# A planned attention and feed-forward kernel: small VectorE operations go to GpSimd and ScalarE, and the planner counts VectorE's waits for GpSimd

## The chip, the core and the metric

The kernel runs on one core of a Trainium2 chip. A core has a matrix engine (TensorE, PE in the profile), VectorE (DVE), ScalarE (ACT), GpSimd (POOL) and SyncE (SP), which issues the transfers. Each engine takes its instructions in the order in which they were written, and waits on semaphores for what other engines make. The metric is device time of one execution, in microseconds (us); lower is better.

## The reference

Three stages, 4608 tokens of 512 numbers:

```
k_p, v_p = means of k, v over 8 neighbours          # 576 -> 72 places, 8 batches, 8 heads of 64
attn = softmax(q @ k_p.T / 8) @ v_p                 # the row sum gets + 1e-9
x = attn as 4608 x 512
h = x @ w_in                                        # 512 -> 1024
solu = h * softmax(h)
ln = (solu - mean) / sqrt(var + 1e-6) * g_ln
y = ln @ w_out                                      # 1024 -> 512
h2 = y @ w2_in                                      # 512 -> 2048
out = (h2 * sigmoid(1.702 * h2)) @ w2_out           # 2048 -> 512
```

## The kernel before

The program has two parts that follow each other on PE. The **first part** does attention, the first feed-forward stage with its norm, and the splitting of all weights. The **second part** does the last feed-forward stage over 12 blocks of 384 tokens; nothing of it is touched here, and its products go to `bank_a`, `bank_b` and `bank_d`.

Products are made in float16 from a high and a low half, so each float32 operand is scaled by a power of two, cast (`hi`), and subtracted (`lo`). The powers of two come from a small chain: largest magnitude of a tile per partition (`am`), spread over partitions by putting it on a diagonal (`diag = eye * am`) and multiplying by ones on PE, a maximum over the row (`alln`), the exponent bits (`pw`), and a few one-column operations (`rc`, `up`, `dn`). Function `largest` holds the diagonal, `whole_scale` and `wide_scale` the one-column operations.

The first part works on 36 tiles of 128 tokens. For each tile `attention` loads `qt`, multiplies it with the pooled keys (`kbd`) into the bank `psx`, takes the row maxima (`mx`), subtracts and exponentiates (`e`), sums the rows (`rs`: a reduction, a scaling `(rs + 1e-9) / A_TOP`, a reciprocal), normalises `e`, splits it into `st`, turns it by a transposing transfer (`aT`), multiplies with the values (`vst`) into the one bank `psv`, and reads that bank twice, on ACT and on DVE, into `xT`. `Pair.hidden` multiplies `xT` with `w1i` into `psh` (two buffers), and makes `hmx`, `nm`, `he`, `tt`, the sum `sm`, the `mean` and the sum of squares `vs`. `Pair.norm` makes, for two tiles together, on 128x2 values, the factor `a` and the shift `mean` of the norm: `q`, `v`, then a power -0.5 on GpSimd (`r`), one correcting step (`q`, `q`, `a`), `mean`. ACT then applies `a` and `mean` to `tt`, casts it (`zs`), GpSimd subtracts the low half, and a transposing transfer makes `zT`, which `project` multiplies with `w1o` into `psy`. Between these, the weights of the last stage are loaded (`raw`), joined from 64-bit input, combined (`w_f`), split and stored.

The order of the first part's instructions isn't written out. Each piece of work is a strand of operations with a due time, and `Plan.run` builds the order: at each step it estimates when the next operation of each strand could start, from its own model of engine costs (`cost`) and of latencies between engines, and writes out the one with the lowest start, shifted a little by its due time. `V`, `G`, `A` put an operation on DVE, POOL, ACT; `VG` lets the plan choose between POOL and DVE. So a cost in the model changes the order on every engine. Due times and their constants (`STEP`, `LAG_PROJECT` and others) stay as they are. Almost all first-part vector work is recorded under one helper line, L472, and its products under L501; the names of the tiles tell the operations apart.

Of the kernel before, what the change touches and what calls it, by code (L numbers as in the profile page):

```python
# [13 lines left out]
ALU = mybir.AluOpType  # L14
# [62 lines left out]
TOP3 = 2.0 ** -29 * (1 - 2.0 ** -23)  # L77
A_TOP = 2.0 ** 14
LN_UP = 2.0 ** 10
SQ_DOWN = 1.0 / (LN_UP * math.sqrt(DF1))  # L80
V_MOST = 2.0 ** 100
Y_TOP = 2.0 ** 13
G_DOWN = 2.0 ** -22
TINY = 2.0 ** -100
# [15 lines left out]
class Op:  # L100


    def __init__(self, engines, emit, outs, ins, cost, turn=False):
        self.engines, self.emit, self.cost, self.turn = engines, emit, cost, turn
        self.outs, self.ins = ([Region(x) for x in xs] for xs in (outs, ins))


# [65 lines left out]
class Plan:  # L173
# [7 lines left out]
    def __init__(self):  # L181
        self.free = dict.fromkeys(("pe", "dve", "act", "pool", "sp", "dma", "none"), 0.0)
        self.uses, self.floor, self.rings, self.ring_of = {}, {}, {}, {}
        self.strands, self.now, self.warm = [], None, 0.0

    def start(self, steps, due):
        s = Strand(self, steps, due)
# [16 lines left out]
    def drop(self, *tiles):  # L204
        for t in tiles:
            del self.ring_of[t.name]
# [12 lines left out]
    def estimate(self, op):  # L219
        best = None  # L220
        for engine in op.engines:
            t = max(self.free[engine], self.ready(op, engine))
            if engine == "sp":
                t = max(t, self.free["dma"] - 2000)
            key = t + op.cost[engine] + self.spare[engine] if len(op.engines) > 1 else t
            if best is None or key < best[0]:
                best = (key, t, engine)
        return best[1:]

    def take(self, op, t, engine):  # L230
        if engine == "sp":
            begin = max(self.free["dma"], t + (1275 if op.turn else 1100))
            self.free["dma"] = end = begin + op.cost["sp"]
            self.free["sp"] = max(t + 625, end - 920) if op.turn else t + 520
            engine = "dma"
        elif engine == "none":
            return
        else:
            cost = op.cost[engine]
            if engine == "pe":  # L240

                gap = t - self.free["pe"]
                self.warm = 0.0 if gap > 3400 else self.warm if gap < 300 or self.warm > 3400 else 0.0
                if self.warm < 3400:
                    cost = min(2 * cost, 3400 - self.warm + max(0.0, cost - (3400 - self.warm) / 2))
                self.warm += cost
            self.free[engine] = end = t + cost
        for regions, writes in ((op.ins, False), (op.outs, True)):
            for r in regions:
                u = self.uses.setdefault(r.name, [])  # L250
                u[:] = [x for x in u if not (x[1] == writes and x[0].box == r.box and x[3] == engine)]
                u.append((r, writes, end, engine))
# [25 lines left out]
def moe_kernel(ctx: ExitStack, tc: tile.TileContext, qT, kT, vT, w_in, w_out, g_ln, w2_in, w2_out, eye, outT):  # L278
# [135 lines left out]
    with ExitStack() as ph:  # L414
# [54 lines left out]
        def op(engines, name, args, kw):  # L469
            def emit(engine):  # L470
                eng = {"dve": nc.vector, "pool": nc.gpsimd, "act": nc.scalar}[engine]
                getattr(eng, name)(*args, **kw)  # L472

            kw_out = [kw[k] for k in ("out", "accum_out") if k in kw]
            outs = aps(kw_out or args[:1])
            ins = aps([v for k, v in kw.items() if k not in ("out", "accum_out")] + list(args[0 if kw_out else 1 :]))
            return Op(engines, emit, outs, ins, {e: cost(e, name, outs, ins) for e in engines})

        def V(name, *args, **kw):
            return op(("dve",), name, args, kw)  # L480
# [49 lines left out]
        def largest(am, alln, least, early=True):  # L530


            if early:
                diag = yield New(sb, [P, P], F32, "diag0", "y", 2)
            else:
                diag = yield New(kv, [P, P], F32, "diag", bufs=1)
            yield V("tensor_scalar", out=diag, in0=eye_t, scalar1=am, scalar2=least, op0=ALU.mult, op1=ALU.max)
            yield there(diag)
            if early:
                ps = yield New(psy, [P, 2, YB], F32, "psy", "psy")  # L540
            else:
                ps = yield New(psv, [P, DM], F32, "psv", "psv")
            spread = ps[:, 0, :P] if early else ps[:, :P]
            yield T([(spread, ones, diag, True, True)])
            drop(diag)
            yield V("tensor_reduce", out=alln, in_=spread, axis=AX.X, op=ALU.max)
            drop(ps)

        def exponent(pw, alln):
            yield V(  # L550
# [17 lines left out]
        def wide_scale(alln, up, dn, there_now):  # L568
            pw, rc = s1("pw", 1, KM), s1("rc", 1, KM)
            yield from exponent(pw, alln)  # L570
            yield V("reciprocal", rc, pw)
            yield V("tensor_scalar_mul", up, rc, 2.0 ** -111)
            there_now.add((up.name, up.offset))
            yield V("tensor_mul", rc, pw, pw)
            yield V("tensor_mul", rc, rc, rc)
            yield V("scalar_tensor_tensor", out=dn, in0=rc, scalar=2.0 ** -8, in1=rc, op0=ALU.mult, op1=ALU.mult)

        def values_of(raw, up, dst, begun=None):

# [28 lines left out]
        def whole_scale(alln, up, dn):  # L608

            pw, rc = s1("pw", 1, KM), s1("rc", 1, KM)  # L610
            yield from exponent(pw, alln)
            yield V("reciprocal", rc, pw)
            yield V("tensor_mul", rc, rc, rc)
            yield V("tensor_mul", rc, rc, rc)
            yield V("scalar_tensor_tensor", out=up, in0=rc, scalar=2.0 ** 8, in1=rc, op0=ALU.mult, op1=ALU.mult)
            yield V("reciprocal", dn, up)

        def joined(raw, measured):
# [141 lines left out]
        def keys(b, due):  # L760
            kp = yield from pooled("k", b, kT, due)
            yield lambda: b < 2 or scored[last_tile(b - 2)]
            for j in range(2):
                r = slice(j * D64, (j + 1) * D64)
                yield V(
                    "tensor_scalar_mul", kbd[b % 2][r, :, j * SP : (j + 1) * SP], kp[r],
                    1.0 / (NPOOL * math.sqrt(D64)),
                )
            drop(kp)
            k_ready[b] = True  # L770

        def values(b, due):
# [17 lines left out]
            v_ready[b] = True  # L790
            yield w_in_done.over
            both = s1("v_sc", 2)
            yield V(
                "scalar_tensor_tensor", out=both[:, 0:1], in0=dn, scalar=1.0 / NPOOL, in1=w1i_dn, op0=ALU.mult,
                op1=ALU.mult,
            )
            yield V(
                "scalar_tensor_tensor", out=both[:, 1:2], in0=up, scalar=float(NPOOL), in1=w1i_up, op0=ALU.mult,
                op1=ALU.mult,
            )  # L800
            for t in range(NTILE):
                for o, n, tb in spans(t):
                    if tb == b:
# [3 lines left out]
        def attention(t):  # L807
# [40 lines left out]
                yield A(out=e, in_=e, func=AF.Exp)  # L848
            rs = s1("rs", H)
            yield V("tensor_reduce", out=rs, in_=e, axis=AX.X, op=ALU.add)  # L850
            yield V("tensor_scalar", out=rs, in0=rs, scalar1=1e-9, scalar2=1.0 / A_TOP, op0=ALU.add, op1=ALU.mult)
            yield V("reciprocal", rs, rs)
            yield VG("tensor_tensor", out=e, in0=e, in1=rs.unsqueeze(2).to_broadcast([P, H, SP]), op=ALU.mult)
            yield lambda: t < 2 or turned[t - 2]
# [40 lines left out]
        class Pair:  # L895
# [7 lines left out]
            def hidden(self, j):  # L903
# [10 lines left out]
                for k in range(KM):  # L914
# [26 lines left out]
                    accum_out=self.mean[:, s],  # L941
                )
                drop(ps)
                yield V("tensor_scalar_mul", self.mean[:, s], self.mean[:, s], -SQ_DOWN / DF1)
                yield A(
                    out=e, in_=tt, func=AF.Square, scale=SQ_DOWN, bias=self.mean[:, s], accum_out=self.vs[:, s]
                )
                drop(e)
                self.tt[j] = tt

            def norm(self):
# [3 lines left out]
                self.a = a  # L955


                tiny = 1e-6 * DF1 * SQ_DOWN ** 2
                yield V("scalar_tensor_tensor", out=q, in0=self.sm, scalar=1e-9, in1=self.ci, op0=ALU.add, op1=ALU.mult)
                yield V("scalar_tensor_tensor", out=q, in0=q, scalar=tiny, in1=q, op0=ALU.mult, op1=ALU.mult)  # L960
                yield V("scalar_tensor_tensor", out=v, in0=q, scalar=V_MOST, in1=self.vs, op0=ALU.min, op1=ALU.add)
                yield G("tensor_tensor", out=r, in0=v, in1=minus_half, op=ALU.pow)
                yield V("tensor_mul", q, r, r)
                yield V("scalar_tensor_tensor", out=q, in0=q, scalar=-0.5, in1=v, op0=ALU.mult, op1=ALU.mult)
                yield V("scalar_tensor_tensor", out=a, in0=q, scalar=1.5, in1=r, op0=ALU.add, op1=ALU.mult)
                yield V(
                    "scalar_tensor_tensor", out=self.mean, in0=self.mean, scalar=1.0 / SQ_DOWN, in1=a, op0=ALU.mult,
                    op1=ALU.mult,
                )
                yield lambda: self.i == 0 or pairs[self.i - 1].zT is not None  # L970
                self.zT = yield New(sb, [P, 2 * K1, YB], F16, "zT", "zT", 2)
                for j in range(2):
# [501 lines left out]
```

## Time and profile before

| | us |
|---|---|
| median of 3 runs (lowest, highest) | 1301.56 (1301.0, 1302.12) |
| the profiled execution | 1298.91 |
| its span, first to last instruction | 1297.1 |
| granted TensorE clock, mean share of full speed | 0.975 |
| busy: PE, DVE, ACT, POOL | 1160.6, 823.3, 753.0, 638.1 |

"Busy" is the time in which at least one instruction of the engine ran. PE's time is a modelled one, since matmuls overlap. A releaser is what ended an engine's idle time; "issue" is idle time for which the profile shows none.

### The profile page before, as it was taken

Reading aid. Unit: us, or ns where it says so; the run is one execution under the profiler, and the core shown is the slowest. Engines: PE = TensorE matmul, PEld = TensorE weight load, DVE = VectorE, ACT = ScalarE, POOL = GpSimd, SP = SyncE. Lnnn points to the kernel's source line nnn. Section 1 sums busy time; section 2 is a strip of 40 time slices with the busy share of each in tenths; the row PEclk is TensorE's granted clock in tenths of the full one; section 3 lists DMA queues with packets and bytes.
Section 4 is the critical chain, followed back from the end, with each engine's and each line's share of the span. In section 5 each row is a group of like instructions: output and inputs, shape, how many; then the busy total and the mean of one; then the engine's idle time right before and its main releaser. Section 6 shows DMA issues by size and latency. Waiting matters only on the chain.

```text
span 1297.1 us, 27516 instructions
## 1 busy us (share of the span) xinstructions
PE 1160.6 (89%) x11678; PEld 996.9 (77%) x11678; DVE 823.3 (63%) x1315; ACT 753.0 (58%) x1009; POOL 638.1 (49%) x541
## 2 busy tenths in 40 slices
PE   2677899888889989899999999999999999999998
PEld 2335566555555656588999999999999999999998
DVE  8999987698988685414454727364554637273633
ACT  6887767677677676435453725454453636364543
POOL 5875846677876585313341526152333415252431
PEclk9989899999899999999999999999999999999999
DMA  9979996987999649926010010101010100101000
GB/s 325 274 223 206 264 233 173 203 218 192 243 267 248 127 118 232 268 74 260 14 38 25 26 32 26 44 8 44 14 38 14 38 26 26 50 8 44 9 18 25
DMA packets 246523, 152.85 MB, mean 118 GB/s; under 512 B 163584, under 2 KB 226176, under 8 KB 244096
## 3 DMA queue, kind: packets, MB, share of 16 engines
q1 hardware_dynamic: 246400, 151.09, 44.0%
q8 instruction: 91, 1.49, 0.5%
q14 instruction: 32, 0.26, 0.1%
HBM read 77.66 MB, written 33.55 MB: 86 GB/s over the span
## 4 chain that ended last, share of the span: by engine, by line
PE 37%; DVE 29%; POOL 13%; ACT 11%; issue 7%; DMA 1%; SPq 1%; ACTq 0%; POOLq 0%; DVEq 0%
PE bank_a L1284 17%; PE bank_d L1284 7%; ACT w_g L1319 6%; DVE g L1331 5%; PE psy L501 5%; PE psh L501 5%; POOL w_g L333 3%; POOL w_g L332 3%; DVE raw L472 2%; POOL w_g L330 2%; PE bank_b L1284 2%; DVE q L472 2%; DVE tt L472 2%; POOL w_g L331 2%; DVE rs L472 2%
## 5 line engine op out<-in xcount | busy, mean ns | idle before, releaser
L1284 PEld LDWEIGHTS <-w2i 128*128 128x128 f16 x4032 | 334.7, 98 | 30.5 <-issue 30.3
L1284 PEld LDWEIGHTS <-w2o 128*128 128x128 f16 x4032 | 334.9, 98 | 8.2 <-issue 7.5
L1284 PE MATMUL bank_a<-ys,w2i 128*128 128x192 f16 x2304 | 213.7, 246 | 24.2 <-ACT c L1294 22.1
L330 POOL TENSOR_TENSOR w_g<-w_g 128x384 f32<-128x384 f32 x36 | 44.2, 1227 | 375.2 <-ACT w_g L1319 375.2
L501 PE MATMUL psh<-w1i,xT 128*128 128x512 f16 x864 | 211.5, 398 | 9.5 <-DVE rs L472 3.7
L501 PE MATMUL psy<-zT,w1o 128*128 128x256 f16 x1728 | 202.3, 277 | 7.4 <-ACT y L472 6.3
L1284 PE MATMUL bank_a<-g,w2o 128*128 128x192 f16 x2304 | 206.1, 246 | 1.1
L501 PEld LDWEIGHTS <-w1o 128*128 128x128 f16 x1728 | 171.1, 99 | 37.3 <-issue 9.7
L1331 DVE SCALAR_TENSOR_TENSOR g<-w_g,gu_b,g 128x1152 f16<-128x1152 f32 (+1 forms) x96 | 168.5, 1775 | 25.3 <-ACT g L1328 25.2
L501 PEld LDWEIGHTS <-xT 128*128 128x128 f16 x864 | 85.7, 102 | 109.5 <-issue 21.2
L1294 ACT ACTIVATE c<-bank_a 128x384 f32<-128x384 f32 x192 | 91.6, 484 | 111.9 <-PE bank_a L1284 110.2
L1328 ACT ACTIVATE g<-w_g,gu_b 128x1152 f16<-128x1152 f32 (+1 forms) x96 | 132.8, 1407 | 38.4 <-POOL w_g L333 38.0
L1297 DVE SCALAR_TENSOR_TENSOR c<-bank_d,c 128x384 f32<-128x384 f32 x96 | 53.3, 555 | 132.2 <-ACT c L1294 97.8
L472 POOL TENSOR_TENSOR zs<-tt,zs 128x1024 f16<-128x1024 f32 x36 | 77.3, 2147 | 78.2 <-ACT zs L472 78.0
L1284 PE MATMUL bank_d<-ys,w2i 128*128 128x192 f16 x1152 | 105.5, 247 | 0.0
L1284 PE MATMUL bank_d<-g,w2o 128*128 128x192 f16 x1152 | 102.5, 246 | 3.3 <-DVE g L1331 3.3
L1319 ACT ACTIVATE w_g<-c,ch_b 128x1536 f32<-128x1536 f32 x48 | 75.3, 1568 | 36.7 <-DVE c L1297 36.6
L1294 ACT ACTIVATE c<-bank_a,co_b 128x384 f32<-128x384 f32 x47 | 26.9, 573 | 108.5 <-PE bank_a L1284 108.5
L501 PE MATMUL psx<-kbd,qt 128*128 128x144 f32 (+1 forms) x320 | 50.0, 325 | 31.5 <-issue 14.6
L501 PEld LDWEIGHTS psx<-kbd,qt 128*128 128x128 f32 (+1 forms) x320 | 44.2, 206 | 36.9 <-issue 33.1
L472 POOL TENSOR_TENSOR lo<-w_f,hi 128x512 f16<-128x512 f32 (+1 forms) x48 | 64.6, 1364 | 12.3 <-ACT hi L472 7.6
L1297 DVE SCALAR_TENSOR_TENSOR c<-bank_b,c 128x384 f32<-128x384 f32 x48 | 26.7, 556 | 63.6 <-ACT c L1294 46.8
(181 smaller groups left out, 1761.7 us busy)
## 6 DMA issues: line engine op xcount, KB each, us to landing
raw<-w_out SPq DMA_DIRECT2D x12, 1024.0 KB, 6.9
raw<-w_in SPq DMA_DIRECT2D x10, 1024.0 KB, 9.0
half<-kT SPq DMA_DIRECT2D x16, 576.0 KB, 5.3
half<-vT SPq DMA_DIRECT2D x16, 576.0 KB, 5.6
qt<-qT SPq DMA_DIRECT2D x36, 256.0 KB, 3.3
y_dram<-y SPq DMA_DIRECT2D x36, 256.0 KB, 2.7
y<-y_dram SPq DMA_DIRECT2D x48, 192.0 KB, 3.3
outT<-c SPq DMA_DIRECT2D x48, 192.0 KB, 1.9
```

Source lines behind the costliest of these rows:

```text
L330: eng.tensor_tensor(out=w[:, 1], in0=q[:, Q12], in1=q[:, Q11], op=ALU.subtract)
L331: eng.tensor_tensor(out=w[:, 2], in0=q[:, Q22], in1=w[:, 1], op=ALU.subtract)
L332: eng.tensor_tensor(out=w[:, 0], in0=q[:, Q22], in1=q[:, Q12], op=ALU.subtract)
L333: eng.tensor_tensor(out=w[:, 3], in0=q[:, Q21], in1=w[:, 2], op=ALU.subtract)
L472: getattr(eng, name)(*args, **kw)
L501: nc.tensor.matmul(*p[:3], start=p[3], stop=p[4])
L1284: nc.tensor.matmul(bank[:, q], self.weight(p, q, kk, w), self.data(p, kk, i), start=(first and q == 0 and kk == 0 and w == 0 and i == 0), ...
L1294: nc.scalar.activation(out=self.c[:, i], in_=bank, func=AF.Copy, scale=self.scale)
L1297: nc.vector.scalar_tensor_tensor(out=self.c[:, i], in0=bank, scalar=self.scale, in1=self.c[:, i], op0=ALU.mult, op1=ALU.add)
L1319: nc.scalar.activation(out=self.w[:, 0:4], in_=self.c, func=AF.Gelu_apprx_sigmoid, scale=self.ch)
L1328: nc.scalar.activation(out=self.g[:, 0, s], in_=self.w[:, s], func=AF.Copy, scale=self.gu)
L1331: nc.vector.scalar_tensor_tensor(out=self.g[:, 1, s], in0=self.w[:, s], scalar=self.gu, in1=self.g[:, 0, s], op0=ALU.mult, op1=ALU.subtract,)
```

## The change

On the side of the operations: the first part's power-of-two chains use one-column `tensor_scalar` forms in place of products of two tensors; the diagonal, the scaled keys and the scaling of the row sums are made by ACT; the norm's 128x2 arithmetic is made by GpSimd, in ten operations in place of seven on DVE and one on GpSimd, with its scale factors put elsewhere and clamps on the factors of `v_sc`. On the side of the planner: a DVE operation that is marked `port` (it reads SBUF alone, and a tensor or several columns) is taken to start no earlier than the end of the GpSimd operation that is running; an ACT operation with an accumulator costs 190 ns more, a power 550 ns more.

```diff
@@ -77,8 +77,7 @@
 TOP3 = 2.0 ** -29 * (1 - 2.0 ** -23)
 A_TOP = 2.0 ** 14
 LN_UP = 2.0 ** 10
-SQ_DOWN = 1.0 / (LN_UP * math.sqrt(DF1))
-V_MOST = 2.0 ** 100
+CI_LEAST, CI_MOST = 2.0 ** -50, 2.0 ** 40
 Y_TOP = 2.0 ** 13
 G_DOWN = 2.0 ** -22
 TINY = 2.0 ** -100
@@ -100,8 +99,8 @@
 class Op:
 
 
-    def __init__(self, engines, emit, outs, ins, cost, turn=False):
-        self.engines, self.emit, self.cost, self.turn = engines, emit, cost, turn
+    def __init__(self, engines, emit, outs, ins, cost, turn=False, port=False):
+        self.engines, self.emit, self.cost, self.turn, self.port = engines, emit, cost, turn, port
         self.outs, self.ins = ([Region(x) for x in xs] for xs in (outs, ins))
 
 
@@ -181,7 +180,7 @@
     def __init__(self):
         self.free = dict.fromkeys(("pe", "dve", "act", "pool", "sp", "dma", "none"), 0.0)
         self.uses, self.floor, self.rings, self.ring_of = {}, {}, {}, {}
-        self.strands, self.now, self.warm = [], None, 0.0
+        self.strands, self.now, self.warm, self.pool_from = [], None, 0.0, 0.0
 
     def start(self, steps, due):
         s = Strand(self, steps, due)
@@ -222,6 +221,8 @@
             t = max(self.free[engine], self.ready(op, engine))
             if engine == "sp":
                 t = max(t, self.free["dma"] - 2000)
+            if engine == "dve" and op.port and self.pool_from <= t < self.free["pool"]:
+                t = self.free["pool"]
             key = t + op.cost[engine] + self.spare[engine] if len(op.engines) > 1 else t
             if best is None or key < best[0]:
                 best = (key, t, engine)
@@ -245,6 +246,8 @@
                     cost = min(2 * cost, 3400 - self.warm + max(0.0, cost - (3400 - self.warm) / 2))
                 self.warm += cost
             self.free[engine] = end = t + cost
+            if engine == "pool":
+                self.pool_from = t
         for regions, writes in ((op.ins, False), (op.outs, True)):
             for r in regions:
                 u = self.uses.setdefault(r.name, [])
@@ -474,7 +477,15 @@
             kw_out = [kw[k] for k in ("out", "accum_out") if k in kw]
             outs = aps(kw_out or args[:1])
             ins = aps([v for k, v in kw.items() if k not in ("out", "accum_out")] + list(args[0 if kw_out else 1 :]))
-            return Op(engines, emit, outs, ins, {e: cost(e, name, outs, ins) for e in engines})
+
+            sides = [x for x in ins if count(x) > 1 or name == "tensor_tensor"]
+            port = (
+                name in ("tensor_tensor", "tensor_mul", "scalar_tensor_tensor", "tensor_scalar", "tensor_scalar_add",
+                         "tensor_scalar_mul")
+                and bool(sides) and all(x.space != PSUM for x in ins)
+            )
+            extra = 190 * ("accum_out" in kw and engines == ("act",)) + 550 * (kw.get("op") == ALU.pow)
+            return Op(engines, emit, outs, ins, {e: cost(e, name, outs, ins) + extra for e in engines}, port=port)
 
         def V(name, *args, **kw):
             return op(("dve",), name, args, kw)
@@ -534,7 +545,7 @@
                 diag = yield New(sb, [P, P], F32, "diag0", "y", 2)
             else:
                 diag = yield New(kv, [P, P], F32, "diag", bufs=1)
-            yield V("tensor_scalar", out=diag, in0=eye_t, scalar1=am, scalar2=least, op0=ALU.mult, op1=ALU.max)
+            yield A(out=diag, in_=eye_t, func=AF.Copy, scale=am)
             yield there(diag)
             if early:
                 ps = yield New(psy, [P, 2, YB], F32, "psy", "psy")
@@ -545,6 +556,7 @@
             drop(diag)
             yield V("tensor_reduce", out=alln, in_=spread, axis=AX.X, op=ALU.max)
             drop(ps)
+            yield V("tensor_scalar_max", alln, alln, least)
 
         def exponent(pw, alln):
             yield V(
@@ -571,9 +583,9 @@
             yield V("reciprocal", rc, pw)
             yield V("tensor_scalar_mul", up, rc, 2.0 ** -111)
             there_now.add((up.name, up.offset))
-            yield V("tensor_mul", rc, pw, pw)
-            yield V("tensor_mul", rc, rc, rc)
-            yield V("scalar_tensor_tensor", out=dn, in0=rc, scalar=2.0 ** -8, in1=rc, op0=ALU.mult, op1=ALU.mult)
+            yield V("tensor_scalar_mul", rc, pw, pw)
+            yield V("tensor_scalar_mul", rc, rc, rc)
+            yield V("tensor_scalar", out=dn, in0=rc, scalar1=rc, scalar2=2.0 ** -8, op0=ALU.mult, op1=ALU.mult)
 
         def values_of(raw, up, dst, begun=None):
 
@@ -610,9 +622,9 @@
             pw, rc = s1("pw", 1, KM), s1("rc", 1, KM)
             yield from exponent(pw, alln)
             yield V("reciprocal", rc, pw)
-            yield V("tensor_mul", rc, rc, rc)
-            yield V("tensor_mul", rc, rc, rc)
-            yield V("scalar_tensor_tensor", out=up, in0=rc, scalar=2.0 ** 8, in1=rc, op0=ALU.mult, op1=ALU.mult)
+            yield V("tensor_scalar_mul", rc, rc, rc)
+            yield V("tensor_scalar_mul", rc, rc, rc)
+            yield V("tensor_scalar", out=up, in0=rc, scalar1=rc, scalar2=2.0 ** 8, op0=ALU.mult, op1=ALU.mult)
             yield V("reciprocal", dn, up)
 
         def joined(raw, measured):
@@ -762,9 +774,9 @@
             yield lambda: b < 2 or scored[last_tile(b - 2)]
             for j in range(2):
                 r = slice(j * D64, (j + 1) * D64)
-                yield V(
-                    "tensor_scalar_mul", kbd[b % 2][r, :, j * SP : (j + 1) * SP], kp[r],
-                    1.0 / (NPOOL * math.sqrt(D64)),
+                yield A(
+                    out=kbd[b % 2][r, :, j * SP : (j + 1) * SP], in_=kp[r], func=AF.Copy,
+                    scale=1.0 / (NPOOL * math.sqrt(D64)),
                 )
             drop(kp)
             k_ready[b] = True
@@ -790,14 +802,10 @@
             v_ready[b] = True
             yield w_in_done.over
             both = s1("v_sc", 2)
-            yield V(
-                "scalar_tensor_tensor", out=both[:, 0:1], in0=dn, scalar=1.0 / NPOOL, in1=w1i_dn, op0=ALU.mult,
-                op1=ALU.mult,
-            )
-            yield V(
-                "scalar_tensor_tensor", out=both[:, 1:2], in0=up, scalar=float(NPOOL), in1=w1i_up, op0=ALU.mult,
-                op1=ALU.mult,
-            )
+            c, ci = both[:, 0:1], both[:, 1:2]
+            yield V("tensor_scalar", out=c, in0=dn, scalar1=1.0 / NPOOL, scalar2=w1i_dn, op0=ALU.mult, op1=ALU.mult)
+            yield V("tensor_scalar", out=ci, in0=up, scalar1=w1i_up, scalar2=CI_LEAST, op0=ALU.mult, op1=ALU.max)
+            yield V("tensor_scalar_min", ci, ci, CI_MOST)
             for t in range(NTILE):
                 for o, n, tb in spans(t):
                     if tb == b:
@@ -848,7 +856,7 @@
                 yield A(out=e, in_=e, func=AF.Exp)
             rs = s1("rs", H)
             yield V("tensor_reduce", out=rs, in_=e, axis=AX.X, op=ALU.add)
-            yield V("tensor_scalar", out=rs, in0=rs, scalar1=1e-9, scalar2=1.0 / A_TOP, op0=ALU.add, op1=ALU.mult)
+            yield A(out=rs, in_=rs, func=AF.Copy, scale=1.0 / A_TOP, bias=1e-9 / A_TOP)
             yield V("reciprocal", rs, rs)
             yield VG("tensor_tensor", out=e, in0=e, in1=rs.unsqueeze(2).to_broadcast([P, H, SP]), op=ALU.mult)
             yield lambda: t < 2 or turned[t - 2]
@@ -941,10 +949,8 @@
                     accum_out=self.mean[:, s],
                 )
                 drop(ps)
-                yield V("tensor_scalar_mul", self.mean[:, s], self.mean[:, s], -SQ_DOWN / DF1)
-                yield A(
-                    out=e, in_=tt, func=AF.Square, scale=SQ_DOWN, bias=self.mean[:, s], accum_out=self.vs[:, s]
-                )
+                yield V("tensor_scalar_mul", self.mean[:, s], self.mean[:, s], -1.0 / DF1)
+                yield A(out=e, in_=tt, func=AF.Square, bias=self.mean[:, s], accum_out=self.vs[:, s])
                 drop(e)
                 self.tt[j] = tt
 
@@ -955,18 +961,18 @@
                 self.a = a
 
 
-                tiny = 1e-6 * DF1 * SQ_DOWN ** 2
-                yield V("scalar_tensor_tensor", out=q, in0=self.sm, scalar=1e-9, in1=self.ci, op0=ALU.add, op1=ALU.mult)
-                yield V("scalar_tensor_tensor", out=q, in0=q, scalar=tiny, in1=q, op0=ALU.mult, op1=ALU.mult)
-                yield V("scalar_tensor_tensor", out=v, in0=q, scalar=V_MOST, in1=self.vs, op0=ALU.min, op1=ALU.add)
+                e0 = NPOOL * math.sqrt(1e-6 * DF1)
+                k = LN_UP * math.sqrt(DF1)
+                yield G("tensor_scalar", out=q, in0=self.sm, scalar1=1e-9, scalar2=e0, op0=ALU.add, op1=ALU.mult)
+                yield G("tensor_tensor", out=q, in0=q, in1=self.ci, op=ALU.mult)
+                yield G("tensor_tensor", out=q, in0=q, in1=q, op=ALU.mult)
+                yield G("tensor_tensor", out=v, in0=q, in1=self.vs, op=ALU.add)
                 yield G("tensor_tensor", out=r, in0=v, in1=minus_half, op=ALU.pow)
-                yield V("tensor_mul", q, r, r)
-                yield V("scalar_tensor_tensor", out=q, in0=q, scalar=-0.5, in1=v, op0=ALU.mult, op1=ALU.mult)
-                yield V("scalar_tensor_tensor", out=a, in0=q, scalar=1.5, in1=r, op0=ALU.add, op1=ALU.mult)
-                yield V(
-                    "scalar_tensor_tensor", out=self.mean, in0=self.mean, scalar=1.0 / SQ_DOWN, in1=a, op0=ALU.mult,
-                    op1=ALU.mult,
-                )
+                yield G("tensor_tensor", out=q, in0=r, in1=r, op=ALU.mult)
+                yield G("tensor_tensor", out=q, in0=q, in1=v, op=ALU.mult)
+                yield G("tensor_scalar", out=q, in0=q, scalar1=-0.5 * k, scalar2=1.5 * k, op0=ALU.mult, op1=ALU.add)
+                yield G("tensor_tensor", out=a, in0=q, in1=r, op=ALU.mult)
+                yield G("tensor_tensor", out=self.mean, in0=self.mean, in1=a, op=ALU.mult)
                 yield lambda: self.i == 0 or pairs[self.i - 1].zT is not None
                 self.zT = yield New(sb, [P, 2 * K1, YB], F16, "zT", "zT", 2)
                 for j in range(2):
```

## Rows read from the trace of the kernel before

**Rows 1.** Stretches: us; busy us (instructions) of five engines; PEclk, DMA share, GB/s.
```profile
0.00:588.50 588.50, 482.90 (x3620) 329.14 (x3621) 463.98 (x849) 409.45 (x603) 378.30 (x353) 0.95 0.85 214
588.50:1297.10 708.60, 677.74 (x8061) 667.74 (x8059) 359.30 (x467) 343.54 (x406) 259.79 (x188) 1.00 0.11 38
0.00:40.00 40.00, 16.10 (x64) 11.28 (x64) 33.56 (x57) 27.37 (x50) 23.66 (x32) 1.00 0.94 320
40.00:480.00 440.00, 369.56 (x2787) 245.17 (x2788) 389.03 (x709) 327.33 (x481) 311.73 (x291) 0.94 0.88 214
160.00:480.00 320.00, 279.74 (x2149) 190.41 (x2144) 273.94 (x488) 229.81 (x335) 224.71 (x210) 0.96 0.84 204
480.00:588.50 108.50, 97.24 (x771) 72.69 (x770) 41.38 (x85) 54.75 (x74) 42.90 (x32) 0.97 0.68 178
```

**Rows 2.** Three slices of 40 us, the same columns.
```profile
160.00:200.00 40.00, 36.83 (x295) 25.39 (x290) 32.20 (x56) 26.89 (x38) 20.24 (x21) 0.96 0.85 212
320.00:360.00 40.00, 32.08 (x255) 22.09 (x254) 37.35 (x66) 29.17 (x44) 32.61 (x34) 0.90 1.11 257
400.00:440.00 40.00, 38.63 (x306) 27.27 (x304) 26.00 (x50) 26.53 (x39) 24.01 (x21) 1.00 0.76 186
```

**Rows 3.** PE's waits to 588.5 us: us in total, times, longest us.
```profile
PE psv L501 <- DVE xT L472: 24.6, 11, 5.1
PE psx L501 <- DMA qt<-qT: 12.2, 1, 12.2
PE psv L501 <- DVE nm L472: 0.8, 1, 0.8
```

**Rows 4.** The chain that ended last, 40 to 480 us, by line.
```profile
by line: issue 9.9%; PE psh L501 8.9%; DVE raw L472 6.8%; DVE q L472 5.6%; DVE tt L472 5.5%; DVE rs L472 4.5%; DVE e L472 4.0%; PE psy L501 3.9%; DVE hmx L472 3.1%; DVE xT L472 2.8%; DVE mx L472 2.8%; DVE rc L472 2.4%; DVE diag L472 2.3%; P
```

**Rows 5.** Timeline near 260 us: start us, us, engine, operation [idle before].
```profile
260.08 2.13 POOL L472 TENSOR_TENSOR zs<-tt,zs 128x1024 f16<-128x1024 f32 x1 [0.57 <-ACT zs L472]
260.10 2.13 DVE L472 TENSOR_TENSOR rc<-pw 128x1 f32<-128x1 f32 x1
```

**Rows 6.** Operations by tile: duration ns min/median/max, first and last start us.
```profile
L472 DVE TENSOR_SCALAR rs<-rs x36: 154/172/2089, 18.8 to 488.4; 128x8 f32<-128x8 f32 x36
L472 DVE TENSOR_SCALAR mean<-mean x36: 136/145/154, 61.7 to 553.4; 128x1 f32<-128x1 f32 x36
```

**Rows 7.** DVE's operations on `q` (108), then `diag` (20): busy us.
```profile
0.00:588.50 588.50, 55.30 (x108) 0.95 0.85 214
0.00:588.50 588.50, 15.94 (x20) 0.95 0.85 214
```

**Rows 8.** DVE's groups by form: busy us, mean ns, idle before.
```profile
L472 DVE SCALAR_TENSOR_TENSOR mean<-mean,a 128x2 f32<-128x2 f32 x18 | 5.6, 314 | 0.4
L472 DVE TENSOR_SCALAR rs<-rs 128x8 f32<-128x8 f32 x36 | 15.5, 432 | 0.5
L472 DVE TENSOR_SCALAR kbd<-kp 64x288 f32<-64x288 f32 x16 | 8.3, 522 | 0.2
L472 DVE TENSOR_TENSOR rc<-pw 128x1 f32<-128x1 f32 x8 | 8.5, 1067 | 0.2
L472 DVE TENSOR_TENSOR rc<-rc 128x1 f32<-128x1 f32 x12 | 6.3, 527 | 0.2
```

**Rows 9.** Short POOL operations: duration ns min/median/max.
```profile
L472 POOL COPY h_sc<-v_sc x40: 176/186/702, 30.3 to 463.4; 128x2 f32<-128x2 f32 x32, 64x2 f32<-64x2 f32 x8
L472 POOL TENSOR_TENSOR kp<-half x1: 447/447/447, 8.2 to 8.2; 128x144 f32<-128x144 f32 x1
L472 POOL TENSOR_TENSOR r<-v,half_power x18: 690/702/1157, 83.8 to 555.2; 128x2 f32<-128x2 f32 x18
```

**Rows 10.** Short ACT operations: ns min/median/max; busy us, mean ns, idle before.
```profile
L472 ACT ACTIVATE e<-psx,mx x8: 313/334/363, 16.0 to 17.4; 128x72 f32<-128x72 f32 x8
L472 ACT ACTIVATE xT<-psv 128x512 f16<-128x512 f32 x36 | 21.1, 585 | 16.4 <-PE psh L501 12.0 <-PE psv L501 4.4
```

**Rows 11.** An ACT wait: us in total, times, longest us.
```profile
ACT he L472 <- DVE mean L472: 27.5, 17, 3.2
```

## The prediction, made before the changed kernel was run

> **What bounds the kernel now.** I read the table of stretches first. The program has two parts, and TensorE (PE) runs them one after the other: the last first-part product and the first `bank_a` product meet at 588.5 us [rows 1]. The reader is to see that in the second part, 708.6 us, PE is busy for 677.7; the diff touches nothing there, so I carry it over unchanged. The question is how far the 588.5 us of the first part shrink.
>
> There PE is busy 482.9 us and idle for 105.6. By stages (same rows): 23.9 idle in the first 40 us, where loads and the first scales have to come; 440.0 - 369.6 = 70.4 between 40 and 480 us; 11.3 in the closing 108.5, where PE has held-back `psy` products to do and DVE is busy only 41.4 us. The closing stage is PE's own. The middle one is not: there VectorE (DVE) is busy 389.0 of 440 us, 88%, against ACT 74% and GpSimd (POOL) 71%.
>
> Next come single slices of 40 us [rows 2]. With DVE at 93%, PE reaches 80%; with DVE at 80 and 65%, PE reaches 92 and 97%. PE does well where DVE has room.
>
> Third, the waits and the chain. Of PE's waits in the first part, twelve rows name DVE as releaser, from `psv <- xT`, 24.6 us, to 0.8; together 63.3 us [rows 3]. In the chain of waits between 40 and 480 us, the names that this change thins stand with `q` 5.6%, `rs` 4.5%, `rc` 2.4%, `diag` 2.3% [rows 4]: 14.8% of 440, 65 us, of which part of `rs` (its reduction and reciprocal) stays.
>
> **Why small operations are dear here.** A product of one column against itself (`rc<-pw`) took 2.13 us; it began 20 ns after a 2.13 us GpSimd operation and ended 20 ns after it [rows 5]. The eight-column `rs` scaling has a median of 172 ns and a maximum of 2089, whereas the one-column `tensor_scalar` on `mean`, 36 times, never left 136 to 154 [rows 6]. So DVE forms with two tensor inputs, or with several columns, can stand and wait for a running GpSimd operation; one-column `tensor_scalar` does not. The planner of before knows nothing of that, so its order on PE was made for a DVE faster than the real one.
>
> **The change, part by part.** Durations are totals of the profiled execution, waits included.
>
> 1. The norm steps. Seven DVE operations for each of 18 pairs go: six forms under `q`, `v`, `a`, 55.3 us [rows 7], and the last on `mean`, 5.6 [rows 8]: 60.9 us off DVE. Nine new GpSimd operations on 128x2 take their place beside the power. No row shows such a product. Below: the 176 ns minimum of the 128x2 copy; above: the 447 ns of a 128x144 product; nearest in size is the copy, 186 ns at the median [rows 9]. 162 operations make 29 to 72 us; I take 30. Behind them on POOL stand the subtractions that feed the transposing loads, and PE after those: their cover is POOL's idle time, 128 of the 440 us. The power's step to POOL and back goes; I book nothing for that.
> 2. The `rs` scaling to ACT: 36 x 432 ns = 15.5 us off DVE [rows 8]. ACT gets 36 short ones; an activation of 128x72 takes 334 ns [rows 10], and this has 8 columns: from nothing to 12 us, I take 0.25 each, 9.
> 3. `diag` to ACT: 20 operations, 15.9 us [rows 7], of which the one that belongs to the second part's first block stays on DVE; 19/20 make 15.1. 19 one-column maxima at 0.15 (the `mean` row) come back, 2.9: net 12.2. `kbd` to ACT: 8.3 us off [rows 8]. On ACT these 35 lie between 334 ns and the 585 ns of a 128x512 copy [rows 10]; at 0.4 that is 14 us. With `rs` ACT gets 23 us (12 to 32), under its idle 113 of 440.
> 4. The 20 `rc` products become one-column `tensor_scalar`: 8.5 + 6.3 us [rows 8] become 20 x 0.15 = 3.0: 11.8 saved. The like forms on `v_sc`, up and down scales are a few each; I book them at nothing, the extra clamps against the lost waits.
>
> Sum: 60.9 + 15.5 + 12.2 + 8.3 + 11.8 = 108.7 us off DVE's 464.0. Some of that was waiting which the next two-input operation now meets instead (`raw` stays); I give back 9 and count 100. The planner's port rule should hold part of the waits down by picking other work first; I book nothing for it, as a new order can also fall worse. Its higher price for the power is what the rows show, 702 ns against a copy's 186 [rows 9].
>
> **The sum.** The middle stage has 84% of DVE's time (389.0 of 464.0), so 84 of the 100 us leave it: 305 of 440, 69%. That is between the two light slices, 65 and 80%, where PE was at 97 and 92%. I take the lower, 92%, because POOL and ACT grow: 369.6 / 0.92 = 402 us, 38 less. Start and close I leave as they are. The profiled execution took 1298.9 us (span 1297.1); 1298.9 - 38 = 1261. The median of the runs lies 2.65 above that execution: 1301.6 - 38 = **1264 us**. At 97% the stage would be 381, 59 less: 1243, and with 5 off the start 1238. At 88% it would be 420, 20 less: 1282.
>
> A page weighs against the main edit. The Trainium skill, GPSIMD Engine Reference, section 4.1, sends elementwise work on a tile to VectorE and calls GPSIMD about twice as slow for two inputs. No row here shows the two-column product. An estimate by its factor is 2 x 0.15 = 0.30 us an operation, 49 us on POOL in place of 30, which would put the time near the dear case of the first rival.
>
> **Rivals.**
>
> *POOL or ACT takes over.* POOL's middle stage grows from 311.7 by 0.84 x 30 = 25 to 337; ACT's from 327.3 by 19 to 346. In a stage of 402 us that is 84 and 86%, and both run in order, so a short step now waits behind subtractions of over 2 us [rows 5]. In the slice shown where POOL is fullest it is at 82% (32.61 of 40) [rows 2]. At the copy's price 337 / 0.82 = 411, 29 less: 1273. Halfway between copy and 128x144 product, at 0.32 us, it is 355 / 0.82 = 433, 7 less: 1295. For: both engines lie close. Against: DVE ran that slice at 93%, and the operations that may go to either engine can go to DVE when POOL is late.
>
> *Slower: the `rs` step stalls DVE.* Reduction, scaling and reciprocal were all on DVE; now DVE's reciprocal waits for ACT, and behind it stand the DVE reads of PE's banks (`hmx`, `mx`, `xT`), for which PE waits. A like step, from DVE's `mean` to ACT's `he`, costs 27.5 us over 17 waits, 1.6 each [rows 11]. 36 x 1.6 = 58 against the 38 gained: 1322. It decides from 38 / 36 = 1.06 us of bare standing each. Against: the planner counts the step and can put other DVE work between, and ACT is free a quarter of the time.
>
> *The transfers keep the pace.* The DMA share is 0.88 over the middle and 1.11 in one slice [rows 1, 2]. If the stretch up to 160 us, which holds 70.4 - 40.3 = 30 of the idle time, can't shrink, only the rest gains: 279.7 / 0.92 = 304 from 320, 16 less, 1286. Against: PE's largest wait for a DMA is one of 12.2 us, for `qt` [rows 3], and that is at the start.
>
> *It does nothing:* the new order is unlucky by as much as the lighter DVE gives, 1299 to 1304.
>
> **How the numbers follow.** Forecast, 1243 to 1282: 0.62. More than that: 0.05. POOL or ACT, 1273 to 1295: 0.14. Transfers, about 1286: 0.08. Nothing: 0.03. Slower: 0.08. A measurement here can tell about 0.2%, 2.6 us. Faster 0.62 + 0.05 + 0.14 + 0.08 = 0.89, same 0.03, slower 0.08. The range goes from the 97% case with the start, 1238, to the dear POOL, 1295; it leaves out the slower case, no change and part of the "more".
>
> **What would show it.** Right: the first `bank_a` product near 550 us; DVE busy 355 to 375 us in the first part; `rc` forms at 150 ns with no long maximum; POOL at 400 to 415; PE's waits for DVE below 40 us. Wrong: DVE waiting over 1 us for each `rs` on ACT; POOL above 84% in the middle with PE waiting for what it makes; PE's idle time there at 70 us still, under other releasers; or DMAs named before `qt`, `aT`, `raw`.

## The result, and the profile after

The changed kernel took 1254.6 us (median of 4 runs, 1251.9 to 1256.1) against 1301.6 us before: ratio 0.9636, 95% interval 0.9619 to 0.9653, so 47 us or 3.6% faster. The forecast was 1264 us in a range of 1238 to 1295: the side is right, the time is inside the range, and the gain was taken some 9 us too small. The profiled execution took 1253.3 us, its span is 1251.5.

The stretches of the changed kernel, with the columns of [rows 1]; the first part now ends at 539 us:

```profile
0.00:539.00 539.00, 462.36 (x3616) 318.87 (x3617) 370.37 (x686) 422.87 (x667) 403.81 (x508) 0.98 0.92 235
539.00:1251.50 712.50, 681.10 (x8062) 670.74 (x8061) 360.55 (x467) 343.60 (x407) 260.86 (x188) 0.99 0.11 37
40.00:440.00 400.00, 361.37 (x2856) 242.38 (x2857) 308.24 (x585) 347.93 (x555) 341.56 (x421) 0.97 0.97 239
400.00:440.00 40.00, 39.04 (x330) 27.77 (x328) 31.06 (x62) 34.57 (x53) 39.69 (x53) 1.00 0.70 171
```

Against [rows 1] the first part lost 49.5 us and the second gained 3.9. In the first part DVE fell from 464.0 to 370.4 us busy, ACT rose from 409.5 to 422.9, POOL from 378.3 to 403.8. PE's idle time fell from 105.6 to 76.6 us, 29 less; and PE's busy time fell too, from 482.9 to 462.4, with the same products (3620 and 3616 records). The mean granted clock beside it went from 0.95 to 0.98 of full speed. The clock has two levels, 2.4 and 1.2 GHz. In the first part the low one was granted for 61 us before, with PE busy in 51 of them, and for 24 us after, with PE busy in 15. If a product takes twice as long at the low level, 25 us were lost before and 7.5 after. That is an estimate of 18 of the 20.5 us by which PE's busy time fell.

The two levels can be seen side by side at the start of the second part, in 3.4 us of the changed kernel and 3.4 us of the kernel before, with products of the same shape:

```profile
540.10:543.50 3.40, 3.40 (x24) 3.13 (x22) 0.00 (x0) 0.49 (x1) 0.00 (x0) 0.50 0.95 290
```
```profile
589.10:592.50 3.40, 3.40 (x44) 3.40 (x42) 0.56 (x1) 1.08 (x3) 0.00 (x0) 1.00 1.02 281
```

PE got through 24 products at 1.2 GHz and through 44 at 2.4. Shortly before, it had stood 3.4 us waiting for ACT in the first case and 1.1 us in the second.

In the middle PE is busy 90% of 400 us, with DVE at 77, ACT at 87 and POOL at 85%. In the last row POOL is at 99%, and PE at 98.

PE's waits up to 540 us, the longest of 16 rows (us in total, times, longest):

```profile
PE psv L512 <- DMA aT<-st: 12.9, 4, 7.3
PE psx L512 <- ACT raw_z L475: 12.7, 1, 12.7
PE psv L512 <- DVE xT L475: 10.3, 5, 5.2
PE psy L512 <- ACT y L475: 8.8, 5, 3.0
PE psh L512 <- DVE mean L475: 8.2, 4, 3.7
```

The row on top in [rows 3], 24.6 us for DVE's `xT`, is down to 10.3. All rows that name DVE make 25.7 us where they made 63.3. The first wait of all, 12 us, only has another name now. New in size is the wait for the turned attention (`aT`), 12.9 us.

The small operations by tile (ns, min/median/max) and, for the new ones on POOL, two rows of the stretch view (us busy) for `q` with `v` and `a`, and for `mean`:

```profile
L475 DVE TENSOR_SCALAR rc<-pw x8: 213/214/215, 108.5 to 415.9; 128x1 f32<-128x1 f32 x8
L475 DVE TENSOR_SCALAR rc<-rc x12: 203/214/216, 28.3 to 416.9; 128x1 f32<-128x1 f32 x12
L475 ACT ACTIVATE rs<-rs x36: 188/198/210, 21.1 to 434.0; 128x8 f32<-128x8 f32 x36
L475 POOL TENSOR_TENSOR q<-q,h_sc x18: 192/197/644, 80.9 to 503.7; 128x2 f32<-128x2 f32 x18
```
```profile
0.00:539.00 539.00, 32.97 (x144) 0.98 0.92 235
0.00:539.00 539.00, 3.98 (x18) 0.98 0.92 235
```

The reader is to see the maxima: the one-column products, which had reached 2.13 us [rows 5], end at 216 ns. The nine new operations cost POOL 33.0 + 4.0 = 37.0 us.

### The profile page after: what moved, and what is told of

The parts are those of the page before. It is cut to its first block, busy times and chain, and to the rows that moved or that the text cites. A ratio compares the mean times of both kernels' runs of the same rounds, so it can differ in the third digit from the quotient of the medians.

```text
span 1251.5 us, 27586 instructions
## 1 busy us (share of the span) xinstructions
PE 1143.5 (91%) x11678; PEld 989.6 (79%) x11678; DVE 730.9 (58%) x1153; ACT 766.5 (61%) x1073; POOL 664.7 (53%) x696
## 4 chain that ended last, share of the span: by engine, by line
PE 30%; POOL 12%; DVE 8%; ACT 8%; issue 5%; DMA 0%; ACTq 0%; POOLq 0%
PE bank_a L1290 18%; PE bank_d L1290 8%; ACT w_g L1325 6%; DVE g L1337 5%; POOL w_g L336 3%; PE bank_b L1290 3%; POOL w_g L335 3%; POOL w_g L333 2%; POOL w_g L334 2%; PE psy L512 2%; ACT g L1334 1%; DVE c L1303 1%; POOL zs L475 1%; DVE w_g L333 0%; ACT c L1300 0%
## 5 line engine op out<-in xcount | busy, mean ns | idle before, releaser
L512 PE MATMUL psh<-w1i,xT 128*128 128x512 f16 x864 | 205.8, 389 | 8.9 <-DVE mean L475 8.2
L512 PE MATMUL psy<-zT,w1o 128*128 128x256 f16 x1728 | 196.8, 273 | 8.8 <-ACT y L475 8.8
L512 PEld LDWEIGHTS <-w1o 128*128 128x128 f16 x1728 | 167.9, 98 | 35.8 <-issue 10.3
L512 PE MATMUL psx<-kbd,qt 128*128 128x144 f32 (+1 forms) x320 | 46.3, 306 | 24.6 <-ACT raw_z L475 12.7
L512 PEld LDWEIGHTS psx<-kbd,qt 128*128 128x128 f32 (+1 forms) x320 | 41.4, 193 | 29.4 <-issue 12.7
L475 DVE TENSOR_REDUCE hmx<-psh 128x1 f32<-128x1024 f32 x36 | 43.7, 1214 | 34.1 <-PE psh L512 34.1
```

The source lines that it names most:

```text
L512: nc.tensor.matmul(*p[:3], start=p[3], stop=p[4])
```

## The experiments

Twelve kernels in three lots; each ratio is to the kernel before, run on the same chip in the same lot (its medians there were 1302.3, 1300.4 and 1300.9 us). Three theories are kept apart. *Load*: what pays is work and waiting taken off DVE. *Order*: what pays is that the planner knows of the waits. *Luck*: the order fell well. Gains in us are worked out from the ratios.

**Operations and planner apart.** The changed operations with the planner of before:

```diff
-            if engine == "dve" and op.port and self.pool_from <= t < self.free["pool"]:
-                t = self.free["pool"]
...
-            extra = 190 * ("accum_out" in kw and engines == ("act",)) + 550 * (kw.get("op") == ALU.pow)
+            extra = 0
```

> The changed operations, but the planner without the port rule and without the 190 and 550 ns. Theory load (what pays is the work and the waiting taken off VectorE): 1262 us, at least four fifths of the 47 us stay. Theory order (what pays is that the plan now knows of the waits): 1285 us or more. Theory luck (the order fell well): anything, with the same VectorE busy time as the changed kernel.

1266.7 us, ratio 0.9719 (0.9693 to 0.9745): 37 of the 47 us, just short of the four fifths that *load* asked for. The opposite, the operations of before with the changed planner (the same lines put into the old kernel, with the one-column products of two tensors marked as `port` too):

> The operations of before, planned with the port rule (two-tensor forms of one column counted as port users too) and with the 190 and 550 ns. Theory load: within 10 us of 1301.6. Theory order: 1275 us or less, with VectorE's long maxima gone.

1274.2 us, ratio 0.9788 (0.9754 to 0.9822): 28 us. Load and order each pay a good part alone, and together less than their sum of 65. The long maximum of `rs` stayed (2115 ns), that of the `rc` products fell from 2130 to 683; DVE's busy time in the first part fell to 438.1 us with as many operations on it (850 and 849). So neither theory holds alone.

**The same split with the order held.** In the next two, each operation takes the place in the order that its counterpart had, and only what is written out differs; the sequences of PE and of the transfers are then the same: in the traces they agree by the names of the tiles. First the changed operations in the old order:

```diff
+        def like(planned, *made):
+            # takes its place in the order as `planned` would, and writes out `made`
...
-            yield A(out=rs, in_=rs, func=AF.Copy, scale=1.0 / A_TOP, bias=1e-9 / A_TOP)
+            yield like(
+                V("tensor_scalar", out=rs, in0=rs, scalar1=1e-9, scalar2=1.0 / A_TOP, op0=ALU.add, op1=ALU.mult),
+                A(out=rs, in_=rs, func=AF.Copy, scale=1.0 / A_TOP, bias=1e-9 / A_TOP),
+            )
```

> The changed operations written out in exactly the order that the planner of before made for the operations of before: PE and the transfers have the same sequence as before. Theory load: PE's waits for VectorE shrink in the old order too, 1270 to 1285 us. Theory order: GpSimd's and ScalarE's queues were laid out for other work, 1295 us or more.

1272.0 us, ratio 0.979 (0.9756 to 0.9823): 27 to 28 us with no change of PE's order. And the operations of before in the new order (the same `like`, the other way round):

> The operations of before, written out in exactly the order that the changed planner made for the changed operations: PE and the transfers have the same sequence as in the changed kernel. With the changed operations in the old order giving 29 of the 47 us, the two parts add up if this gives 18 (1284 us). If the new order is good by itself: 1275 us or less. If it is only good for a light VectorE: 1295 us or more.

1286.3 us, ratio 0.989 (0.986 to 0.992): 14 us, near the 1284 at which the parts add up. With the order held, the parts are 27 and 14 and make 41 of the 47 us. What is left depends on the way round: the operations give 27 us in the old order and 33 in the new one, the order gives 14 us with the old operations and 20 with the new ones. The first-part row of the changed operations in the old order, up to the first lasting `bank_a` product:

```profile
0.00:558.70 558.70, 472.62 (x3616) 323.12 (x3617) 362.79 (x678) 425.38 (x674) 411.14 (x515) 0.96 0.89 226
```

DVE is lighter there than in the changed kernel itself (362.8 us) and the first part still ends 20 us later: with the load gone, the rest is order.

**Waiting alone.** The kernel before in its own order, with nothing changed but 46 one-column products:

```diff
-            yield V("tensor_mul", rc, pw, pw)
+            yield like(V("tensor_mul", rc, pw, pw), V("tensor_scalar_mul", rc, pw, pw))
```

> The kernel before in its own order, with nothing changed but the rc and v_sc products made as one-column tensor_scalar: as many instructions on the same engine, only their waits for GpSimd go. Theory load: 14 to 16 us off VectorE's busy time, and at the changed kernel's rate (47 us for 94 us of VectorE) 6 to 8 us faster, 1294. If the waits only move to the next two-tensor operation: VectorE's busy time the same, 1300 us or more.

1292.2 us, ratio 0.9931 (0.9911 to 0.995): 9 us, from instructions of the same number on the same engine. DVE's busy time fell by 14:

```profile
0.00:586.00 586.00, 485.54 (x3616) 328.44 (x3617) 449.78 (x849) 410.38 (x603) 378.11 (x353) 0.94 0.87 215
```

The profiled execution was the slowest of ten, 1298.3 us, so this row shows the load and not the gain. The row does show that the waiting went and did not move on to the next two-tensor operation.

**One part put back.** The changed kernel with the norm on DVE (`G` to `V` in nine lines, the power stays), and with the `rs` scaling on DVE (the line of before):

> The changed kernel with the norm's nine small operations back on VectorE, in the new formulas; the power stays on GpSimd. Theory load: the norm was 60.9 of the 108.7 us taken off, so about half of the gain goes, 1275 to 1282 us. Rival, that GpSimd's extra 30 us now hold the time: 1250 us or less.

> The changed kernel with the scaling of the row sums back on VectorE. Theory load: 15.5 us come back to VectorE, 14% of what was taken off, so about 1261 us. Rival, that the step over ScalarE stalls VectorE as much as it saves: 1254 us or less; the changed kernel's trace has a mean of about 1.7 us from the end of the reduction to the end of the reciprocal, with VectorE idle only 2.9 us of it in all, which speaks against.

The norm back: 1265.2 us, ratio 0.9712 (0.9688 to 0.9737), 10 us of gain lost where 20 to 27 were expected. The row of its first part:

```profile
0.00:550.80 550.80, 473.72 (x3616) 326.20 (x3617) 415.35 (x842) 422.84 (x667) 378.52 (x352) 0.96 0.91 229
```

With the norm DVE gets 45 us back, POOL loses 25. The 10 us are the move's net worth in the presence of the others. The `rs` scaling back: 1256.4 us, ratio 0.9644 (0.9617 to 0.967), between its two marks and not to be told from the changed kernel. (The 1.7 us named there is 1.8 by the trace.) DVE's busy time in its first part is not higher (369.7 us) although 36 operations came back, so other waiting shrank; this part of the change can't be seen in the time.

**GpSimd's new load.** Each of the nine small operations a second time, into a scratch tile:

```diff
                 yield G("tensor_tensor", out=q, in0=q, in1=self.ci, op=ALU.mult)
+                yield G("tensor_tensor", out=x2, in0=q, in1=self.ci, op=ALU.mult)
```

> The changed kernel with each of the norm's nine small GpSimd operations made a second time into a scratch tile: 162 more, some 33 us on GpSimd, planned as such. If GpSimd holds the time now: 1270 us or more. If it has room: within 8 us of 1254.6.

1261.5 us, ratio 0.9701 (0.9685 to 0.9717): 7 to 8 us slower than the changed kernel, the edge of "has room". GpSimd's busy time rose by only 20 us, to 423.7. PE's top wait there (columns as above) is now for a transfer that GpSimd feeds, 26.2 us where the changed kernel has 12.9:

```profile
PE psv L512 <- DMA aT<-st: 26.2, 9, 6.4
```

**Luck, and the rest of the planner.** One planner constant moved a little in each kernel (`PULL` 900 to 950), the added costs taken out, and the tiles' pace quickened (`STEP` 12000 to 11000):

> The changed kernel with one planner constant moved a little (PULL 900 to 950), which lays the order out anew without changing any work. Theory luck: over 15 us from 1254.6. Otherwise within 8 us.

> The kernel before with the same constant moved (PULL 900 to 950). Theory luck: over 15 us from 1301.6, towards the changed kernel's time. Otherwise within 8 us.

> The changed kernel without the 190 and 550 ns in the planner's costs, with the port rule. Without both it took 1266.7. If the port rule is what the plan's 12 us come from: 1257 us or less. If the costs are: 1264 or more.

> The changed kernel with the tiles' due times 11 us apart in place of 12, since VectorE can now keep a quicker pace. If the due times hold the lighter engines back: 1248 us or less. If they only break ties: 1251 to 1258.

The moved constant: 1253.4 us after (0.9635, 0.9619 to 0.9651) and 1300.7 before (1.0002, 0.9988 to 1.0017). This says little about luck, because the constant hardly moved the order: by the names of the tiles, PE's products and the transfers follow each other in these traces as without it, in both kernels, and of ACT's sequence 99% or more agrees. The added costs taken out: 1258.9 us, 0.9665 (0.9629 to 0.9701), between its two marks. The interval reaches the changed kernel's, so what these costs give was not settled; the port rule makes most or all of the planner's 11 us. The quicker pace: 1255.3 us, 0.9645 (0.9614 to 0.9676), no change. This kernel does have another order, with 59% of ACT's sequence and 58% of GpSimd's as in the changed kernel when the two traces are matched, and the same time. So luck falls for the changed kernel. Whether the old planner's one order was a bad draw for the old operations, no run shows. None of the twelve beats the changed kernel by more than can be told.

## Why the prediction was right, point by point

- *DVE is what PE waits for in the middle.* Right. In the old order, with only the operations changed, 28 us came; 14 us of waiting alone, on the same engine in the same order, were worth 9. The sign "PE's waits for DVE below 40 us" came: 25.7.
- *109 us off DVE, 9 of them given back, 100 net.* 93.6 measured (464.0 to 370.4). The 20 `rc` products went from 14.8 to 4.3 us, 10.5 saved for the 11.8 booked, as the one-column form costs 214 ns and not 150. Most of what left DVE was waiting: the durations above the fastest tenth of each form sum up to 113 us before and 29 after. The waiting that came back is in few places: eight `e<-e,rs` on DVE took 12.5 us where five had taken 7.1, one of them 5169 ns.
- *POOL 30 us, ACT 23.* The nine operations cost 37.0, at 187 to 197 ns, near the copy's 186 that was taken [rows 9]; the rest of the difference is waits, up to 1.4 us. POOL's total rose by 25.5, since seven operations that may go to either engine went to DVE. ACT: `rs` 36 x 0.20 = 7.2, 19 `diag` at 0.39 = 7.4, 16 `kbd` at 0.44 = 7.0: 21.6 us.
- *PE at 92% in the middle, 402 us, the rest as it was; first part 550.* The mis-sized term. The middle came to 90%, and PE's idle time fell by 29 us in the whole first part where the 92% meant 38; but its busy time, taken as fixed at 369.6 in the middle and 482.9 in all, fell by 20.5, at a granted clock of 0.98 for 0.95. That makes 49.5 for 38. The two errors have opposite signs, so it is in part luck that the forecast of 1264 came so near. That PE ran faster because it stood less is what the rows suggest; no run tells it apart. The split also differs from one execution to the next: the changed kernel with the moved constant, of the same time, had PE idle for 73.2 us and lost 14 to the clock by the estimate above, where the changed kernel itself had 76.6 and 7.5.
- *The second part unchanged.* Nearly: 3.9 us longer. PE's busy time makes 3.4 of that (677.7 to 681.1, at a clock of 0.99 for 1.00). 1.2 GHz was granted there for 10 us in which PE was busy, where it was 3 before, and 3.4 of the 10 stand right at the start, as shown above. PE's wait of 3.4 us for ACT's first `c` (1.1 before), while ACT waited for the store of the last `y`, ends at the seam and counts in the first part.
- *The planner's rule booked at nothing.* Wrong as a step, though within the range: a quarter to two fifths of the gain is order (11 of 47 us between the two planners with the new operations, 14 from the new order with the old operations, 20 with the new ones).

The rivals: *POOL or ACT takes over* is there in part. POOL stands at 85% in the middle, over the 84 that were named as a sign of being wrong, and at 99% in one slice; PE's longest wait in total is for `aT`, which POOL's subtraction feeds; and 20 us more on POOL cost 8. It did not set the time alone, as the norm put back on DVE was worse. On two columns the product took 0.196 us on GpSimd; with the norm back on DVE its medians were 0.155 to 0.186. The estimate by the factor two of the Trainium skill (GPSIMD Engine Reference, section 4.1), 49 us, was too high here. *The `rs` step stalls DVE* did not come in the planned order, and in part in an order that was not planned for it. DVE's waits for the step, changed kernel first, then the changed operations in the old order:

```profile
DVE rs L475 <- ACT rs L475: 2.9, 8, 0.5
```
```profile
DVE rs L477 <- ACT rs L477: 17.3, 26, 3.2
```

The 17.3 us are 0.5 for each of the 36 steps, under the 1.06 at which the prediction would turn, and that kernel was still 27 us faster.

*The transfers keep the pace*: between 40 and 160 us PE's busy time rose from 89.8 to 97.8 us at the same DMA share (0.97 and 0.98), and PE's waits for transfers in the first part came to 18.6 us with 16.1 before; they were no bound. *Nothing* is excluded by the result: the new order was not unlucky.

## What to carry to other kernels

Look at the maximum of an operation's duration, not at its mean: a 0.15 us operation that sometimes took 2.1 was waiting for another engine here, and a form that doesn't wait can be worth more than one that is shorter. When a plan or a hand-made order is built on a cost model, a stall that the model lacks costs twice, once where it happens and once in the order of every other engine; fixing either gives part of the gain, and the parts don't simply add. Before a test by a moved constant counts against luck, compare the two orders: here the constant had moved next to nothing. When the engine that the matrix engine waits for gets lighter, look at the matrix engine's clock as well as at its idle time: here some 18 of the 49.5 us lay there, by an estimate.

## What the runs showed of the hardware that was not expected

First, a DVE operation that waits for GpSimd mostly gets in before GpSimd's next operation, even when that one follows at once, and it is then GpSimd's operation that can be longer. An example from the changed kernel's timeline (start us, us, engine, operation):

```profile
387.41 1.74 POOL L475 TENSOR_TENSOR st<-e,st 128x576 f16<-128x576 f32 x1
387.93 1.84 DVE L475 TENSOR_TENSOR e<-e,rs 128x576 f32<-128x576 f32 x1
389.12 1.24 POOL L475 TENSOR_TENSOR w_f<-w_f 128x256 f32<-128x256 f32 x1
```

The `e<-e,rs`, 0.75 us at its fastest, began while `st` ran and ended 0.62 us after it. The `w_f`, recorded right behind `st`, took 1.24 us where operations of its form take 0.72 at their fastest. In the first part of the changed kernel's trace, 20 times a GpSimd operation followed at once on one for which DVE was waiting; at 18 of them DVE got in, and GpSimd's operation took at least 0.1 us more than its form's fastest. In the kernel before DVE got in at all 78. The other two of the 20 belong to one operation, which stood through three:

```profile
435.98 2.29 POOL L475 TENSOR_TENSOR w_f<-sg,raw 128x512 f32<-128x512 f16 x2
...
437.04 5.17 DVE L475 TENSOR_TENSOR e<-e,rs 128x576 f32<-128x576 f32 x1
438.24 1.27 POOL L475 TENSOR_TENSOR st<-e,st 128x576 f16<-128x576 f32 x1
439.48 2.11 POOL L475 TENSOR_TENSOR zs<-tt,zs 128x1024 f16<-128x1024 f32 x1
```

It began as the first `w_f` of the pair ended, waited through the second, `st` and `zs`, and ended 0.62 us after `zs`. Why this one was not let in, no run shows. The planner's rule counts a wait to the end of the operation that is running, which fits the 18.

Second, a one-column `tensor_scalar` with a column as its factor took 214 ns, where the same with a number takes 145 [rows 6]: dearer than an undisturbed product of two columns (149 ns), but without its waits.
